# One core, chunk-selecting attention with a softplus layer: another order of all operations in the order table

## Chip, cores and metric

One core of one Trainium2 chip runs the whole program. The metric is the device time of one execution in microseconds (us). The kernel before was timed in 3 runs: median 256.69 us, lowest 255.29, highest 258.97. The shares, durations and waits below come from one further execution that the hardware profiler recorded.

## What is computed

Attention over 4 batches, 8 heads, 768 positions and 64 elements per head, in which each query sees only 6 chunks of 32 keys, and then a two-layer network with softplus over the 3072 tokens:

```python
k_min, k_max = k_chunks.min(axis=3), k_chunks.max(axis=3)
ub = sum(maximum(q * k_min, q * k_max), axis=-1)      # bound of each query and chunk
ub = where(causal, ub, -1e9)
top_chunks = argsort(ub, axis=-1)[..., -6:]
scores = where(selected & causal, q @ k.T / 8, -1e9)
attn = softmax(scores)
x = (attn @ v) as 3072 tokens x 512
h = x @ w_in                                          # 512 x 2048
out = softplus(h) @ w_out                             # 2048 x 512
```

Inputs and output are float32 in HBM; the matmuls run on bfloat16.

## The kernel before

The 12 blocks (4 batches, three thirds of 256 positions) go through the same stages, and the stages of neighbouring blocks are mixed on every engine.

- Loads. Block 0's k and q come as float32 halves on SP's queue (L377, tile wx) and are cast on ScalarE or VectorE (L294, L295). All other q, k and v halves (L364), w_in in four pieces (L392) and w_out in four pieces (L399) are issued by GpSimd on the software queue, which converts them to bfloat16 on the way. These issues stand in GpSimd's own instruction stream, between its causal selects (L715) and copies.
- Preparation of a block n. k and q are transposed: on TensorE for blocks 0 to 2 (L481), by DMA transposes on SP from block 3 on (L485). VectorE takes the maximum and minimum of each chunk (L508 from PSUM, L500 from the DMA's tile), writes them into BD (L295) and splits q into its positive and negative part (qpos, qneg: L557 on ScalarE, L559 and L561 on VectorE). TensorE forms the bounds ub (L580, L584). VectorE adds the causal term (L592), finds the sixth largest (L603, L607) and writes the mask (L622, L625). The mask is transposed (L637, L643 on TensorE; L646 by DMA from block 3 on) and copied beside q (L295 or L294, "mc" in the table).
- Attention. Scores on TensorE (L697, L698, "s"), exponential on ScalarE (L705, "ex"), the causal select of the diagonal chunk on GpSimd (L715, "af"), the product with v on TensorE (L727, "av"), normalisation on VectorE (L737, L738, "nm"), then the transposed x by TensorE (L753) or by DMA (L742).
- Network. x times w_in (L891, "h"), softplus as exponential and logarithm on ScalarE (L896, L901), times w_out: plainly for blocks 0 to 3 and 11 (L921, "y"), with seven products of quarter blocks (L836) for blocks 4 to 10. For the seven products sums of parts of w_out are made first (L795, "wd", "wh", "wv", on VectorE or GpSimd). Results leave through SP's queue (L872, L933).

No scheduler decides the order. The string ORDER (L201) lists 1576 words. The first letter of a word is the engine (P TensorE, A ScalarE, V VectorE, G GpSimd, S SyncE), the rest the operation with its block; `#i` picks one of several of the same name. A word `z30` is filler on TensorE: 30 // 4 matmuls of 512 columns and 30 % 4 of 128 columns on a zero tile (L1007, L1009). Each engine runs its own words in the order of the table, and buffers are handed out in that order too (Plan.in_order):

```python
o.eng = {"P": "PE", "A": "ACT", "V": "DVE", "G": "POOL", "S": "SP"}[word[0]]
assert o.eng in o.engines and not o.wait, word
for b in o.alloc:
    _, b.pool, b.slot = min((s.since, p, i) for p in b.pools for i, s in enumerate(p.slots) if not s.taken)
```

A DMA that must wait for another operation waits at its issuing engine, and everything behind it on that engine waits too.

Of the kernel before, what the change touches and what calls it, by code (L numbers as in the profile page):

```python
# [206 lines left out]
Gw_in0 z45 Ps0 Ps0#6 Aex0#6 Aex0 Amc0 z3 Pub1 Ps0#4 Gw_in1 Aex0#4 Vqac1 Vkc1#1 Vmx1 Vraw1 z1 Ps0 Aex0 z16 Ps0 PqT2
PkT2 Ps0 Vqc2 Gaf0#2 Gaf0 Gaf0#4 Gaf0 Vkc1 z4 PmT1 Pav0#2 z12 Pav0#3 Vnm0#1 Gld_v1.0 Gld_v1.1 z14 Pav0 Pav0 Gw_in2
Aex0 Aex0 Amc1 PkT2 Ps1#4 Ps1 PoT0#1 Gld_q3.0 Gaf0 Gaf0 Amc1 Vqpn2 Vqpn2 Vnm0 Aex1#4 z8 Ps1#3 PoT0 Aex1 Aex1#3 Gaf1#1
Gaf0 Gld_q3.1 z2 Ps1#5 Aex1#5 Vkx2 Vkn2 Axc0 Pav0 Pav0 Ps1#7 Aex1#7 Vnm0 Axc0 Vbd2 z4 Ps1#6 Aex1#6 Vkc2 z6 Ps1 Aex1  # L210
Gaf1 Gw_in3 z6 PoT0 Pav0 Pav0 Vnm0 Ps1#8 Ps1#12 Aex1#8 Aex1#12 Pub2 PoT0 Ps1 Vkc2 Axc0#3 Axc0 Vmx2 Vraw2 Ps1 Aex1#9
Aex1 z2 Ph0 Ps1#13 Aex1#13 Pav1 Ps1#14 Aex1#14 Pav1 Gaf1 Ps1#11 PmT2 Ps1#15 Gw_out0 Aex1#11 Ae0 Aex1#15 Gaf1 Vqac2
Vmc2 Gaf1#6 Ph0 Ae0 Ps1 Ps2 Vnm1 Ph0 Aex1 Aex2 Ps2#2 Aex2#2 Vmc2 Gld_v2.0 Gld_v2.1 Pav1 Pav1 PoT1 Gaf1#7 Gld_k3.0
Ps2#6 Vnm1 Ae0 Ps2#5 Aex2#6 Aex2#5 Ph0#4 Ae0#4 Gaf1 Ps2#4 Pav1#6 Ps2#18 Pav1#7 Aex2#18 Aex2#4 Gvone Gld_k3.1 Gaf1
Gw_out1 Gw_out2 Gaf2#1 Ph0#5 Ae0#5 Gw_out3 Gaf2 Vxc1 Vnm1#3 PoT1 SkD3 Pav1 Ps2 PoT1#3 Ps2#23 Ph0 Aex2#23 Aex2 Vxc1 Ae0
Aln0 Ph0 Ps2 Ps2#12 Pav1 Vxc1#3 Vnm1 Aex2 Ph0 Ps2#13 Aex2#12 Ae0 Aex2#13 PoT1 Vxc1 Py0 SqD3 Ae0 Ps2#8 Aln0 Pav2 Ps2#11
# [827 lines left out]
```

## Time and profile before

| | |
|---|---|
| median of 3 runs (lowest to highest) | 256.69 us (255.29 to 258.97) |
| the profiled execution's own time | 256.73 us |
| its span, first to last instruction | 255.0 us |
| TensorE matmul busy | 247.9 us (97%), 2786 matmuls |
| ScalarE, VectorE, GpSimd busy | 215.6, 177.7, 115.6 us (85, 70, 45%) |
| share of 16 DMA engines: software queue, hardware queue | 73.5%, 32.1% |
| granted TensorE clock | 1.00 in every stretch |

A matmul's busy time runs from its issue to its modelled end, so matmuls that follow each other overlap, and the mean duration of one is longer than the distance to the next. Idle time of TensorE is what counts here; idle time of another engine counts only where TensorE waits for it.

### The profile page before, as it was taken

How to read it: one execution, taken by the hardware profiler on the slowest of the kernel's cores; microseconds unless marked ns; L12 is line 12 of the kernel's file. 1: busy time of each engine (PE TensorE's matmuls, PEld its weight loads, DVE VectorE, ACT ScalarE, POOL GpSimd, SP SyncE). 2: the span in 40 equal slices, each digit the busy share in tenths (PEclk: the TensorE clock that was granted, in tenths of full speed). 3: DMA queues.
4: the chain of work that ended last, by engine and by line, in shares of the span. 5: the costliest groups of instructions: out<-in, count | busy, mean ns of one | idle time of the engine just before them, and what ended most of it. 6: DMA issues, size and time to landing. Idle time of an engine off the chain costs nothing.

```text
span 255.0 us, 7155 instructions
## 1 busy us (share of the span) xinstructions
PE 247.9 (97%) x2786; PEld 202.4 (79%) x2786; DVE 177.7 (70%) x562; ACT 215.6 (85%) x396; POOL 115.6 (45%) x196
## 2 busy tenths in 40 slices
PE   6999999999999999999999999999999999999995
PEld 2666798775686777877789999899999988999873
DVE  5899952059899677987898995977765554535501
ACT  3889999987799998997998989999899997767661
POOL 6689791870885774861643732633012213200020
PEclk9999999999999999999999999999999999999999
DMA  7999999999999899999999989568422440200213
GB/s 177 131 111 170 181 195 189 153 116 182 158 134 148 139 172 127 157 146 159 90 162 102 115 152 190 63 50 60 101 66 64 43 146 3 82 3 4 82 44 123
DMA packets 114722, 29.90 MB, mean 117 GB/s; under 512 B 104544, under 2 KB 111712, under 8 KB 114688
## 3 DMA queue, kind: packets, MB, share of 16 engines
q0 software_dynamic: 74944, 13.11, 73.5%
q1 hardware_dynamic: 39744, 16.33, 32.1%
q8 instruction: 22, 0.36, 0.6%
q14 instruction: 12, 0.10, 0.1%
HBM read 27.26 MB, written 6.29 MB: 132 GB/s over the span
## 4 chain that ended last, share of the span: by engine, by line
PE 80%; DVE 9%; DMA 6%; ACT 3%; issue 1%; SPq 0%
PE ph L891 28%; PE py L921 9%; PE pt L836 9%; PE py L836 8%; PE ps L697 5%; DMA qt<-io 5%; PE po L727 5%; PE ps L698 4%; PE pt L727 2%; PE ph L921 2%; PE pt L697 2%; DVE kx L508 2%; PE pt L580 2%; PE pt L698 1%; DMA wx<-in_k_dram 1%; DVE qa L295 1%
## 5 line engine op out<-in xcount | busy, mean ns | idle before, releaser
L891 PE MATMUL ph<-x,w_in_sb 128*128 128x256 bf16 x768 | 97.6, 272 | 0.0
L705 ACT ACTIVATE pt<-ps 128x512 bf16<-128x512 f32 (+1 forms) x151 | 78.1, 551 | 10.0 <-PE ps L698 9.2
L715 POOL TENSOR_SCALAR_AFFINE_SELECT pt<-pt 128x256 bf16<-128x256 bf16 x96 | 39.1, 427 | 98.9 <-ACT pt L705 94.7
L891 PEld LDWEIGHTS <-w_in_sb 128*128 128x128 bf16 x768 | 72.9, 98 | 9.6 <-issue 0.2
L896 ACT ACTIVATE e<-ph 128x512 f32<-128x512 f32 x96 | 56.6, 607 | 8.3 <-PE ph L891 7.9
L901 ACT ACTIVATE g<-e 128x1024 bf16<-128x1024 f32 x48 | 50.5, 1062 | 0.3
L921 PE MATMUL py<-w_out_sb,g 128*128 128x512 bf16 (+1 forms) x144 | 34.0, 367 | 0.0
L727 PEld LDWEIGHTS <-pt 128*128 128x128 bf16 x672 | 27.7, 97 | 2.7
L921 PEld LDWEIGHTS <-g 128*128 128x128 bf16 x176 | 16.2, 97 | 11.1
L705 ACT ACTIVATE pt<-pt 128x512 bf16<-128x512 f32 (+1 forms) x41 | 22.3, 556 | 3.0 <-PE pt L698 2.5
L836 PEld LDWEIGHTS <-g 128*128 128x128 bf16 x224 | 21.0, 98 | 2.3
L727 PE MATMUL po<-v,pt 128*128 128x65 bf16 x468 | 22.5, 193 | 0.0
L500 DVE TENSOR_REDUCE kx<-kT 128x32 bf16<-128x1024 bf16 x18 | 21.3, 1210 | 1.2 <-DMA kT<-io 1.1
L364 POOL DMA_DIRECT2D v<-in_v_dram x24 | 21.4, 895 | 0.2
L364 POOL DMA_DIRECT2D io<-in_k_dram x22 | 20.0, 910 | 0.3
L364 POOL DMA_DIRECT2D io<-in_q_dram x22 | 19.9, 905 | 0.3 <-issue 0.3
L697 PE MATMUL ps<-qt,kb 128*128 128x256 bf16 x76 | 20.0, 272 | 0.0
L697 PE MATMUL ps<-qa,ka 96*128 96x256 bf16 x75 | 19.7, 273 | 0.3 <-DVE qa L295 0.3
L698 PE MATMUL ps<-qt,kb 128*128 128x128 bf16 (+1 forms) x76 | 18.1, 245 | 0.0
L698 PE MATMUL ps<-qa,ka 96*128 96x256 bf16 (+1 forms) x75 | 17.7, 244 | 0.0
L836 PEld LDWEIGHTS <-df 128*128 128x128 bf16 x168 | 15.9, 98 | 2.0
L1007 PE MATMUL py<-zero 128*128 128x512 bf16 x52 | 15.3, 411 | 1.1 <-DVE zero L304 1.1
(127 smaller groups left out, 409.0 us busy)
## 6 DMA issues: line engine op xcount, KB each, us to landing
out_dram<-ysb SPq DMA_DIRECT2D x23, 256.0 KB, 2.3
v<-in_v_dram POOLq DMA_DIRECT2D x24, 128.0 KB, 5.5
io<-in_k_dram POOLq DMA_DIRECT2D x22, 128.0 KB, 5.6
io<-in_q_dram POOLq DMA_DIRECT2D x22, 128.0 KB, 5.4
w_in_sb<-in_moe_w_in_dram POOLq DMA_DIRECT2D x4, 512.0 KB, 8.8
w_out_sb<-in_moe_w_out_dram POOLq DMA_DIRECT2D x4, 512.0 KB, 11.6
wx<-in_k_dram SPq DMA_DIRECT2D x2, 256.0 KB, 3.2
wx<-in_q_dram SPq DMA_DIRECT2D x2, 256.0 KB, 4.3
```

The costliest lines, as they stand in the source:

```text
L364: lambda e, t=t: nc.gpsimd.dma_start(out=into(nm, n, t), in_=rows(nm, n, t)),
L500: nc.vector.tensor_reduce(kx.ap[:, :, j].rearrange("d p (t c) -> d t p c", t=NT), kT.ap.rearrange("d p x -> d (p x)").rearrange("d (t p c ...
L697: nc.tensor.matmul(sp.ap[:, 0:QB], kk[0:nr, p, j * 128:(j + 1) * 128], qq, start=True, stop=True)
L698: nc.tensor.matmul(sp.ap[:, QB:w], kk[0:nr, p, (j + 1) * 128:(j + 2) * 128], qq[:, 1] if last else qq, start=True, stop=True)
L705: lambda e, sp=sp, pt=pt, h=h, j=j, w=w: nc.scalar.activation(pt.ap[:, h, j:j + 2].rearrange("k j c -> k (j c)")[:, 0:w], sp.ap[:, 0:w], A ...
L715: nc.gpsimd.affine_select(out=d, in_=d, compare_op=ALU.is_ge, fill=0.0, base=0, channel_multiplier=-1, pattern=[[0, 2], [1, 128]])
L727: nc.tensor.matmul(o[:, u, h], pt.ap[:, h, j, c0:c0 + 128], T.V[i][:, j, 2 * p + h, :], start=(j == 0), stop=(j == t0 + u))
L836: nc.tensor.matmul(bank.ap[:, c * HD:(c + 1) * HD], a(f), w(f), start=start and f == 0, stop=f == HF - 1, skip_group_check=True)
L891: nc.tensor.matmul(o[:, j], T.w_in[:, dt, ft * 128:(ft + 1) * 128], x.ap[:, dt], start=(dt == 0), stop=(dt == KDM - 1))
L896: lambda e, hb=hb, eb=eb, f2=f2: nc.scalar.activation(eb.ap[:, f2 * 512:(f2 + 1) * 512], hb.ap, ACT.Exp),
L901: lambda e, eb=eb, g=g, f4=f4: nc.scalar.activation(g.ap[:, f4 * 4:(f4 + 1) * 4].rearrange("f j c -> f (j c)"), eb.ap, ACT.Ln, bias=1.0),
L921: nc.tensor.matmul(yb.ap[:, 0:c1 - c0], g.ap[:, f, u * 128:(u + 1) * 128], T.w_out[:, f, c0:c1], start=(f == 0), stop=(f == KFF - 1))
```

## The change

The text of ORDER is replaced; nothing else is. All operations of the old table are in the new one, with the same buffer pools and dependencies; what differs is their order on each engine, which engine does some of them, and the filler. The table now has 1579 words:

```diff
 ORDER = """
-Vzero Vbd0#1 Vcm0 Vkb0 Gident Vr4 Gc4 Sld_k0.1 Vbd0 Vmr0 Gld_k1.0 Gld_q1.0 Sld_k0.0 Acast_k0.0 z30 PkT0 Vmr0 PkT0
-Gld_q1.1 Gld_k1.1 Gcm Gld_q2.0 Gvone Sld_q0.0 Vkx0 Vcast_k0.1 z24 PkT0 PkT0 Vkx0 Vkn0#1 Acast_q0.0 PqT0 PqT0 Aqc0
...
+Vzero Gvone Gident Sld_k0.1 Vkb0 Vmr0#1 Vbd0 Vmr0 Sld_k0.0 Sld_q0.1 Vr4 Gc4 Gld_q1.0 Gvone Vcast_k0.0 z30 PkT0 PkT0
+Vkx0 Vcast_k0.1 z24 PkT0 PkT0 Sld_q0.0 Vkn0 Vkx0 Vkn0 Vcm0 Voh Acast_q0.0 Gld_q1.1 Gld_k1.0 Gld_k1.1 Acast_q0.1 PqT0
...
```

Counted over the table: filler words 22 with a sum of 238 before, 25 with a sum of 231 now, that is 52 matmuls of 512 columns and 30 of 128 before, 48 and 39 now. VectorE has 302 operations before and 310 now, ScalarE 393 and 385, GpSimd 189 and SyncE 95 in both. The first cast of k, three copies of x of block 2 and one or two small copies of the output in blocks 2, 4, 6 and 7 go from ScalarE to VectorE; halves of qpos/qneg and of the mask copies go both ways; the sums of w_out and the last additions of the output trade places between VectorE and GpSimd.

VectorE (DVE), the start of the program, from the constants to the first mask. kx is the tile of chunk maxima and minima of k, io the cast input, ph and pt PSUM tiles, qpos and qneg the parts of q. Before:

```order
L316 COPY rows_67<-ident 128x128
L325 MEMSET bd_76 128x192
L324 MEMSET mraw_78 128x256
L324 MEMSET mraw_79 128x256
L508 TENSOR_REDUCE kx_103<-ph_87 128x2x8
L295 CAST io_97<-wx 128x4x2x64
L508 TENSOR_REDUCE kx_103<-ph_88 128x2x8 x2
L306 SCALAR_TENSOR_TENSOR ohb<-ident 32x768
L508 TENSOR_REDUCE kx_103<-ph_87 128x2x8
L561 TENSOR_SCALAR qpos_109<-qt_106 128x512
L295 COPY kb_74<-ph_88 64x2x256
```

Now:

```order
L316 COPY rows_67<-ident 128x128
L295 CAST io_96<-wx 128x4x2x64
L508 TENSOR_REDUCE kx_103<-ph_87 128x2x8
L295 CAST io_96<-wx 128x4x2x64
L508 TENSOR_REDUCE kx_103<-ph_87 128x2x8
L508 TENSOR_REDUCE kx_103<-ph_88 128x2x8 x2
L310 MEMSET cmask 128x4
L306 SCALAR_TENSOR_TENSOR ohb<-ident 32x768
L561 TENSOR_SCALAR qpos_109<-qt_106 128x512
L295 COPY qa_105<-qt_106 64x512
L295 COPY qt_106<-pt_92 128x512
```

All three memsets of bd and mraw stand ahead of rows now; both casts of k are VectorE's, and the four maxima and minima stand ahead of the one long operation that builds ohb.

GpSimd (POOL), from v of block 1 to the weights. v_70, io_101 and io_102 are the targets of v, q and k halves, pt the probabilities that the causal select works on. Before:

```order
L364 DMA v_70<-in_v_dram 128x8x64 x2
L392 DMA w_in_sb<-in_moe_w_in_dram 128x4x512
L364 DMA io_101<-in_q_dram 128x8x64
L715 AFFINE_SELECT pt_116<-pt_116 128x2x128
L715 AFFINE_SELECT pt_115<-pt_115 128x2x128
L715 AFFINE_SELECT pt_113<-pt_113 128x2x128
L715 AFFINE_SELECT pt_115<-pt_115 128x2x128
L364 DMA io_101<-in_q_dram 128x8x64
L715 AFFINE_SELECT pt_113<-pt_113 128x2x128
L392 DMA w_in_sb<-in_moe_w_in_dram 128x4x512
L715 AFFINE_SELECT pt_114<-pt_114 128x2x128
L399 DMA w_out_sb<-in_moe_w_out_dram 128x4x512
```

Now, from the third k half on:

```order
L364 DMA io_101<-in_k_dram 128x8x64
L364 DMA v_70<-in_v_dram 128x8x64
L715 AFFINE_SELECT pt_115<-pt_115 128x2x128 x2
L399 DMA w_out_sb<-in_moe_w_out_dram 128x4x512
L311 AFFINE_SELECT cmask<-cmask 128x4
L364 DMA io_102<-in_q_dram 128x8x64
L715 AFFINE_SELECT pt_113<-pt_113 128x2x128
L364 DMA io_102<-in_q_dram 128x8x64
L715 AFFINE_SELECT pt_113<-pt_113 128x2x128
L715 AFFINE_SELECT pt_114<-pt_114 128x2x128
L399 DMA w_out_sb<-in_moe_w_out_dram 128x4x512 x2
```

Both q halves of block 3 stood between pieces of w_in; they now stand behind the second piece of w_out. The second and third piece of w_in, further ahead, now stand together behind v of block 1, where the third stands in the rows of before.

VectorE between the mask of block 3 and its copy beside q. wv, wd and wx are the sums of w_out, kx the chunk maxima of block 4, rec and osb the normalisation of block 2, mT the transposed mask. Before:

```order
L625 CAST mraw_79<-ub_112 128x16
L795 TENSOR_TENSOR wd<-w_out_sb 128x512
L795 TENSOR_TENSOR wv<-w_out_sb 128x1024
L795 TENSOR_TENSOR wx<-w_out_sb 128x512
L795 TENSOR_TENSOR wd<-w_out_sb 128x512
L500 TENSOR_REDUCE kx_103<-kT_94 128x2x4x4 x2
L737 RECIPROCAL rec_124<-po_90 128x4
L738 TENSOR_TENSOR osb_123<-po_90,rec_124 128x256
L295 COPY qa_107<-mT_138 32x2x2x128 x2
```

Now:

```order
L625 CAST mraw_79<-ub_112 128x16
L795 TENSOR_TENSOR wv<-w_out_sb 128x1024
L737 RECIPROCAL rec_120<-po_90 128x4
L738 TENSOR_TENSOR osb_119<-po_90,rec_120 128x256
L795 TENSOR_TENSOR wd<-w_out_sb 128x512
L295 COPY qa_107<-qt_108 64x1024
L500 TENSOR_REDUCE kx_103<-kT_94 128x2x4x4 x2
L737 RECIPROCAL rec_124<-po_90 128x4
L738 TENSOR_TENSOR osb_123<-po_90,rec_124 128x256
L295 COPY bd_77<-kx_103 64x8x8 x2
L561 TENSOR_SCALAR qpos_109<-qt_106 128x1024
L295 COPY qa_107<-mT_138 32x2x2x128 x2
```

Two sums have left this stretch; a normalisation, the copy of q, the copies into bd and qpos of block 4 have come in.

## Rows read from the trace of the kernel before

**Rows 1.** TensorE's waits: line waited for: us in total, times, longest.
```profile
PE ph L481 <- ACT io L294: 1.1, 1, 1.1
PE py L1007 <- DVE zero L304: 1.1, 1, 1.1
PE pt L580 <- DVE qneg L559: 0.8, 2, 0.5
PE ps L697 <- DVE qa L295: 0.3, 1, 0.3
PE pt L697 <- DVE qa L295: 0.2, 1, 0.2
PE pt L643 <- DVE mraw L625: 0.2, 1, 0.2
```
**Rows 2.** Busy time by stretch; the first number is the stretch's length.
```profile
core 0: us, PE busy (x) PEld busy (x) DVE busy (x) ACT busy (x) POOL busy (x), PEclk, DMA share, GB/s
10.00:20.00 10.00, 9.67 (x127) 6.62 (x125) 9.55 (x42) 8.93 (x17) 8.83 (x16) 1.00 1.30 113
...
50.00:60.00 10.00, 9.40 (x98) 6.36 (x96) 6.37 (x14) 9.31 (x17) 5.90 (x9) 1.00 2.17 122
...
100.00:120.00 20.00, 20.00 (x260) 16.71 (x257) 17.50 (x55) 17.68 (x33) 11.91 (x20) 1.00 1.56 151
...
240.00:255.00 15.00, 11.96 (x94) 8.94 (x92) 2.48 (x5) 7.00 (x11) 1.45 (x2) 1.00 0.28 106
```
**Rows 3.** The filler: the narrow ones by line, then three stretches of the timeline.
```profile
L1009 PE MATMUL py<-zero 128*128 128x128 bf16 x30 | 4.0, 219 | 0.0
...
5.54 1.46 PE L1007 MATMUL py<-zero 128*128 128x512 bf16 x6
...
14.26 2.55 PE L1007 MATMUL py<-zero 128*128 128x512 bf16 x11
...
17.03 0.33 PE L1009 MATMUL py<-zero 128*128 128x128 bf16 x3
```
**Rows 4.** TensorE's timeline: third h group, bound of block 3, first scores of block 3.
```profile
33.28 1.04 PE L891 MATMUL ph<-x,w_in_sb 128*128 128x256 bf16 x8
...
58.46 0.18 PE L580 MATMUL pt<-bd,qneg 128*128 128x16 bf16 x1 [0.48 <-DVE qneg L559]
...
68.46 0.27 PE L697 MATMUL ps<-qa,ka 96*128 96x256 bf16 x1
```
**Rows 5.** GpSimd's timeline: third w_in piece, second q half of block 3, w_out.
```profile
22.15 0.77 POOL L392 DMA_DIRECT2D w_in_sb<-in_moe_w_in_dram  x1
...
25.77 0.89 POOL L364 DMA_DIRECT2D io<-in_q_dram  x1
...
36.12 1.51 POOL L399 DMA_DIRECT2D w_out_sb<-in_moe_w_out_dram  x2
```
**Rows 6.** DMA issues, us to landing: all w_in; those issued 25.77, 36.12, 44.90.
```profile
w_in_sb<-in_moe_w_in_dram POOLq DMA_DIRECT2D x4, 512.0 KB, 8.8
...
io<-in_q_dram POOLq DMA_DIRECT2D x1, 128.0 KB, 7.8
...
w_out_sb<-in_moe_w_out_dram POOLq DMA_DIRECT2D x1, 512.0 KB, 9.7
...
qt<-io SPq DMA_TRANSPOSE x1, 12.4
```
**Rows 7.** SyncE's timeline: the transpose of q of block 3.
```profile
44.90 4.51 SPq L485 DMA_TRANSPOSE qt<-io  x1
```
**Rows 8.** VectorE's timeline between the mask of block 3 and its copy.
```profile
62.06 0.20 DVE L625 CAST mraw<-ub 128x16 bf16<-128x16 f32 x1
...
63.74 2.35 DVE L500 TENSOR_REDUCE kx<-kT 128x32 bf16<-128x1024 bf16 x2
...
67.44 0.94 DVE L295 COPY qa<-mT 32x512 bf16<-32x512 bf16 x2
```
**Rows 9.** GpSimd's load issues by line, 0 to 64 us: ns min/median/max of one.
```profile
L364 POOL DMA_DIRECT2D io<-in_k_dram x10: 873/893/1054, 3.0 to 52.8; - x10
```

More of the change, by code (lines that the diff above doesn't have):

```diff
@@ L207 @@
[L207 to L216, printed above, removed]
@@ new lines @@
+Gld_v1.0 PqT2 z1 Ps0 Aex0 z7 PmT1 Amc1 Sohk Gld_v1.1 Gaf0 Vqc2 Pav0 z9 Pav0 Vnm0 Amc1 z14 PoT0 Pav0#4 Pav0#5 Vkc1
+Vnm0#2 Ps1#4 Aex1#4 Vqpn2 Ps1#12 PkT2 Aex1#12 Vqpn2 z3 Pav0 Pav0 Vnm0 PkT2 Ps1#6 Gw_in1 Aex1#6 Gw_in2 z4 Ps1#15
+Aex1#15 Gaf0#7 Gaf0 Gaf1#7 Vkx2 Vkn2 z6 Ps1#13 Aex1#13 z3 Ps1#5 z5 Ps1 Aex1#5 z2 Ps1 Gld_k3.0 Pav0 PoT0#2 Pav0 Axc0
+Aex1 Aex1 z4 Ps1 Aex1 Vbd0 Gaf1 PoT0 Vbd2 Ps1#7 Axc0#2 Aex1#7 Vkc2 Gw_out0 Vnm0 z8 Ps1 Pub2 Aex1 PoT0 Ps1 Ps1#11 Vkc2
+Axc0 Axc0 Ph0 Aex1 Vmx2 Gw_in3 Gaf1 Gaf1 Gld_v2.0 Gaf1 Gaf1#6 Aex1#11 Ps1#10 Pav1 Ps1#14 Pav1 Ae0 Vraw2 Vnm1 Aex1#14
@@ new lines @@
+Aex2#23 Ps2 Ph1 Gld_q4.0 Aex2 Ps2#13 Ph1#5 Gld_q4.1 Aln0 Gwh0 Gld_k5.0 Gld_k5.1 Vwh2#1 Ps2 Py0 Aex2#13 Aex2 SkD4
+Ps2#16 Ae1 Aex2#16 Aln0 Ps2 Pav2 Pav2 Vnm2 Ps2#21 Aex2 Ph1#4 Vkx3 Vkn3 Py0 Ps2#22 Vwd0 Aex2#21 Ae1#4 Aex2#22 Ae1#5
+PoT2 Vxc2 Vbd3 Ps2 Pav2 Pav2 Ps2 Vkc3 Vwh6#1 Py0 Ph1 Aye0 Vqpn3 Vkc3 Sohk Py0 Ph1 Py0 Vxc2 Ae1 Aln1 Py0 Aqpn3 Pub3
+Vwv2 Aln1 Py0 Vuba3 Vmx3 Aln1 Aye0 Ph1 Aex2 Vraw3 Gwd2 Gaf2#7 Py1 Py1 Py1 SqD4 Vwv4 Ae1 Ae1 Aln1 Py1 Vnm2 Aex2 SmD3
+Gaf2 Gld_v3.0 Aye1 Vwd4 Vqac3 Vkx4 Pav2 Pav2 Vkn4 Gld_v3.1 PoT2 Axc2 Vnm2 Vbd4 Vqpn4 Sohk Skb0 Py1 Py1 Vmc3 Aqpn4 Pub4
@@ new lines @@
+Py3 Pav5 Vnm5 Vkc7 Ae4 Aex5 Ae4 Ps6 Gaf5 Vqpn7 Vqpn7 Ps6 Ps6#4 Ph4#3 Aex6 Aex6 Aex6 Gaf6 Ps6#6 Aex6#6 Ph4 Ps6 Aex6
+Gaf6#3 Aln3 Pav5 Pav5 Ps6#7 Aex6#7 Pub7 SkD9 Gld_q9.1 Gaf6#6 Vnm5 Vuba7 Vmx7 Vraw7 Py3 Gaf6#7 Gaf6 Gld_q8.0 Ae4 Ae4
+Aln4 Py3 Aye3 Ph4 SxD5 SxD5#3 Gaf6 Ae4 Vqac7 Sst1 SxD5 SxD5 Ps6 Aex6 Aex6 Vkx9 Vkn9 Ph4#6 Pav6#2 Pav6#3 Vnm6#1 Vkc9
+Ae4#6 Ph4#7 Py3 Pav6#6 Pav6 Pav6#7 Vnm6#3 SmD7 Ph4 Aln4 SqD9 Ae4#7 Gaf6#5 Gaf6 Gld_q11.0 Gld_k8.1 Pav6 Gld_k10.0
+Gld_q8.1 Py3 Ph5#4 Vnm6 Vmc7 Vmc7 Vdl4 Ps7#13 Ps7#12 Aln4#3 Ae4 Aln4 Gld_v9.0 Py3 Ps7#8 Ps7#10 Ph5#5 Pav6 Pav6 Aex7#8
@@ new lines @@
+Py5#12 Py5#13 Py5 Py5 Vmc8 Vmc8 Ps8#18 Pav9#5 Aex8#18 Aye5 Vyv5 Vnm9#2 Vyc5 Ph7#6 Ps8#19 Pav9 Pav9 Ps8 Ps8#6 Py5
+Ps8#23 Py5 Aln6 Aex8#6 Aex8 Ps8#2 Vnm9 Ae7#6 Ayd5 SkD10 Vkx10 Vdl6 Vyw5 Vyx5 Aex8#23 Pav9 Aex8#19 Vyf5 Ph7#4 Pav9
+Ps8#12 Ph7 Aex8#2 SqD10 Vde6 Vqpn10 Vqpn10 Vdh6 Vkn10 Vkx11 Ps8#17 Ps8#11 Vnm9 Py6 Ae7 Ps8#5 SxD9 SxD9#3 SxD9 SxD9
+Sst5#1 Aex8#12 Aex8#5 Aex8#11 Ae7#4 Aex8#17 Gaf8#1 Gaf8 Gld_v8.0 Ph7#7 Gld_v8.1 Gld_v11.0 Gaf8#5 Gld_q11.1 Gld_v11.1
+Gaf8#3 Ps8#4 Ps8 Ps8#9 Py6 Py6 Aex8#9 Ps8#14 Aex8 Ps8#22 Ph7#5 Ae7#7 Aex8#4 Aex8#22 Ae7#5 Aex8#14 Py6#4 Py6#5 Ps8#13
```

127 lines of the change are left out of this document (58 added, 69 removed).

## The prediction

> **What bounds the kernel now.** I read the time first: the profiled execution took 256.73 us, of which 255.0 are its span, and the median of the three runs is 256.69, so the sum can be made against 256.73 and taken for the median as it stands. Then the waits of TensorE. They come to 3.7 us in seven waits [rows 1]; 2.2 of these are the start, the zero tile and the first cast of k. Inside the program 1.5 us are left: three waits in the preparation of a block (qneg twice, 0.8; mraw once, 0.2) and two at the first scores of a block, which wait for the mask's copy (0.3 and 0.2). The busy time by stretch says the same from the other side: TensorE is idle 0.33 us of 10 to 20, 0.60 of 50 to 60, nothing of 100 to 120 [rows 2], and 3.04 of the last 15, which is the last copy and store after the last matmul. So TensorE's stream bounds the kernel from end to end, and no other engine counts except where it makes this stream wait. The work in the stream is the same in both tables. What can change is the filler, which is work on TensorE only because the table says so, the waits, and the start and the end.
>
> **The change part by part.**
>
> Filler. Wide fillers come to the same distance in every stretch: eleven take 2.55 us and six take 1.46, so five more take 1.09, 0.218 each. Narrow ones: three take 0.33 and one alone 0.219, so 0.055 each [rows 3]. Before there are 52 and 30, now 48 and 39: 4 x 0.218 less and 9 x 0.055 more, a gain of 0.87 - 0.50 = 0.37 us. A filler runs whether anything is late or not, so this is certain unless its place turns into a wait.
>
> Start. TensorE's first steps are in both tables the same 30, two transposes, 24, and so is the first transfer that they wait for. On VectorE bd and mraw are cleared before rows and not after, so GpSimd's first select and with it its first load come about 0.6 us later; the loads behind it are needed only by block 1. The cast of k that gates the first transposes goes from ScalarE to VectorE at the same length within 0.01 us, and VectorE has nothing else to do then. All maxima are then done before the long ohb operation; in exchange qc of the second half stands on VectorE, and the last q half to be issued is cast first on ScalarE. I take a new wait of 0.25 us at the first bound, between 0 and the 1.1 us that the cast of k costs today [rows 1], because the queue of VectorE is shorter by the maxima and longer by a copy.
>
> Block 1 and 2. The wait of block 1's bound for qneg is 0.3 (0.8 less the longest, 0.5), that of block 2's mask transpose for mraw 0.2 [rows 1]. In the new table one of qpos and qneg of block 1 is ScalarE's and the other is ahead of the maxima on VectorE, and block 2's mask transpose stands behind more scores. Both waits go: 0.5 less. What is late next is the copy of the mask, and the bound is that a wait of the same size comes back, so between 0.5 and 0.
>
> Weights. The second piece of w_in now goes out where the third did, at 22.15 [rows 5]. With the median 8.8 us to landing [rows 6] it is there at 30.95; its first user today, the third h group, starts at 33.28 [rows 4], and stands at the same place in the new stream within 0.6 us (the same filler, 0.37 less, and fewer waits). There is cover of 2 us, and I cost it at nothing; were GpSimd that much later, each us beyond it would be a us of TensorE.
>
> q of block 3. Its second half is issued at 25.77 and lands after 7.8 us, at 33.6, long before SyncE wants it: the transpose of q is issued at 44.90, behind that of k, and lands 12.4 later, at 57.3 [rows 5 to 7]. Then VectorE splits q and TensorE waits until 58.46, 0.48 us [rows 4]. Now the q halves are behind the second piece of w_out and the k halves are ahead of it. If q is on time, the wait stays; TensorE comes 1.0 us later, for one more y group (4 x 0.218 = 0.87) and a score pair stand ahead of the bound, and the split is divided between ScalarE and VectorE. If it is not, that is the first rival. I take no change: nearest to the row of today.
>
> Masks of blocks 3 to 5. VectorE ends the mask at 62.26 and the copy beside q at 68.38; the first scores start at 68.46, so this queue just misses being a wait [rows 4, 8]. The four sums behind the mask take 1.48 us (62.26 to 63.74). In the new order two of them are gone and a normalisation, a copy of q, two small copies and a qpos have come in, each 0.4 to 0.6 by rows of the same kind: some 1.2 us more work, against 0.7 us in which VectorE is idle today and about 1.3 us that the mask starts earlier, since one normalisation and the sums ahead of it have moved. TensorE meanwhile gets there about 1.3 us sooner (one y group, one score pair and two products with v less, one bound more). The two sides come to a wait between 0 and 0.8 us; I take 0.2. At blocks 4 and 5 the 0.5 us of today stays: work between bound and scores grows by 0.3 and shrinks by 0.4.
>
> More on VectorE, less on ScalarE. Eight operations move, some 4 us; in 100 to 120 VectorE is busy 17.50 of 20 and TensorE never waits [rows 2], so nothing is added.
>
> GpSimd's issues beside VectorE. Over the first 64 us ten issues of k halves took 873 to 1054 ns, with 893 in the middle [rows 9], while VectorE was busy 9.55 of 10 us [rows 2]: at worst 0.16 us more for one. The Trainium skill, "SBUF — State Buffer", section "SBUF: two separate sides", says that GpSimd cannot write its descriptors while a VectorE operation holds the port pair that they share; by that each cast or copy moved to VectorE could hold up a load for its whole length. The rows show no such length here, and by the rule the sum would change only if a load were late already.
>
> End. The last two y groups, the last copy and the last store are of the same kinds in the same order. Stores of blocks 8 and 9 now queue behind those of block 10 on SyncE; TensorE's stream ends 3.04 us before the span does in either case. Zero, up to 0.5 if these stores meet the last one.
>
> Sum: 256.73 - 0.37 - 0.5 + 0.25 + 0.2 = 256.3 us.
>
> **The rivals.**
>
> The q halves late (slower). If the software queue delivers in the order of issue, the second q half lands behind the second piece of w_out: 36.12 + 9.7 + 2 x 0.89 = 47.6 [rows 5, 6]. SyncE then issues q's transpose 2.7 us later than at 44.90, and so does all behind it; at 12.4 to landing the bound of block 3 starts at about 61.2 and not 58.46. Of these 2.7 us 1.0 is work that now stands ahead, so the stream is 1.7 behind today's where the forecast has it 0.6 ahead (0.37 + 0.5 - 0.25): price 2.3. With the wait of the block's mask at its upper end, 0.6 more, 256.3 + 2.9 = 259.2. It decides from the point where q lands after 44.90. For it: the order of GpSimd's issues. Against it: all weights start earlier in the new queue, and the 12.4 us may be the price of sharing the engines with weights, which are then nearer their end.
>
> All waits gone (faster). The new places could cover all of the 1.5 us, with no new wait: 256.73 - 0.37 - 1.5 = 254.9. For it: each wait is under 0.5 us, and a single group of matmuls put ahead of it is 0.87. Against it: at blocks 4 and 5 the distance from bound to scores hardly grows.
>
> The change does not do what it says (no difference). The start waits for the first k half and the last q half as before, and waits move rather than go: 256.4 to 257.0. For it: the first transposes, their cast and their transfer are the same on every queue.
>
> **How the numbers follow.** The forecast of 256.3 with its own small terms (255.6 to 256.9) has 0.4, the case of no difference 0.2, all waits gone 0.2, the late q halves 0.15; 0.05 is left for a wait that I have not seen. Two per cent is 5.1 us, about what a measurement of this kernel can tell from no change. A gain of that size would need more than the 0.37 of filler, the 1.5 of waits and the 1.1 of the first cast together: 0.02. A loss of that size needs the late q halves and as much again: 0.06. Within 2%: 0.92. The range goes from 253.8, a little over 1 us below all waits gone for the scatter of the runs (they lie 1.4 below and 2.3 above their median), to 259.7, the late q halves and 0.5 of scatter.
>
> **What would show it right or wrong.** Right: TensorE's waits name no qneg of block 1 and no mraw; wide fillers are 48 at 0.218; TensorE is idle under 0.2 us of 10 to 20; the bound of block 3 starts within 1.5 us of 58.46; the scores of block 3 wait less than 0.8. Wrong: a wait of TensorE over 1 us anywhere after the first cast, above all at L580 with a DMA of io behind it, or h groups waiting for w_in; or a last store that ends more than 3.5 us after the last matmul.

## The result, and the profile after

The changed kernel took 260.38 us (median of six runs, 258.53 to 260.80) beside 256.95 us for the kernel before (six runs, 255.29 to 260.45): a ratio of 1.0112, 95% interval 1.0069 to 1.0155. It is 1.1% slower; by 2% the two count as the same. Ratios and intervals, here and below, leave out the runs more than 1.5% above the fastest of their kernel; medians and ranges take all. The prediction had 256.3 and a range up to 259.7, so time and range were missed. The profiled execution took 260.51 us with a span of 258.8, 3.78 us over the profiled execution before.

TensorE's waits in the changed kernel (answers to [rows 1]; line waited for: us in total, times, longest):
```profile
PE po L727 <- DVE osb L738: 1.2, 2, 0.7
PE pt L697 <- DVE qt L295: 1.1, 1, 1.1
PE py L1007 <- DVE zero L304: 1.1, 1, 1.1
PE ph L481 <- DVE io L295: 0.9, 1, 0.9
PE ps L697 <- DVE qa L295: 0.6, 1, 0.6
PE pt L697 <- DVE qa L295: 0.3, 1, 0.3
PE ph L643 <- DVE mraw L625: 0.2, 1, 0.2
PE pt L753 <- DVE osb L738: 0.2, 1, 0.2
```
The waits at the start come to 2.0 us, 0.2 less than before. The seven others come to 3.6 us where the kernel before had five with 1.5. The qneg waits are gone; new are a wait of 1.1 us for a copy of a mask (qt, L295) and two, 1.2 us together, for a normalisation of VectorE (osb, L738).

The busy time by stretch says where they stand (answers to [rows 2]):
```profile
core 0: us, PE busy (x) PEld busy (x) DVE busy (x) ACT busy (x) POOL busy (x), PEclk, DMA share, GB/s
10.00:20.00 10.00, 10.00 (x126) 6.70 (x125) 8.68 (x37) 8.47 (x15) 7.97 (x12) 1.00 1.37 118
...
50.00:60.00 10.00, 10.00 (x107) 7.13 (x105) 6.79 (x15) 8.69 (x16) 6.03 (x7) 1.00 1.89 168
...
80.00:100.00 20.00, 18.42 (x209) 13.95 (x207) 17.46 (x48) 16.62 (x34) 14.28 (x21) 1.00 1.53 146
100.00:120.00 20.00, 18.64 (x243) 14.86 (x241) 13.22 (x55) 16.62 (x33) 8.71 (x16) 1.00 1.17 119
```
10 to 20 and 50 to 60, where the prediction had counted idle time, are now full. TensorE is idle in 80 to 100 (1.58 us, block 5's scores) where the prediction had let blocks 4 and 5 keep 0.5 us between them, and in 100 to 120 (1.36 us, block 6's), where it had added nothing.

Block 5 in the timeline of the changed kernel (start us, us, engine, line; VectorE, then GpSimd, then TensorE):
```profile
90.35 1.88 DVE L295 COPY qa<-mT 32x512 bf16<-32x512 bf16 x2
92.24 2.47 DVE L295 COPY qt<-mT 32x512 bf16<-32x512 bf16 x2
...
94.97 0.42 DVE L738 TENSOR_TENSOR osb<-po,rec 128x256 bf16<-128x256 f32 x1
...
90.34 1.77 POOL L364 DMA_DIRECT2D v<-in_v_dram  x2
92.11 0.43 POOL L715 TENSOR_SCALAR_AFFINE_SELECT pt<-pt 128x256 bf16<-128x256 bf16 x1
92.47 0.90 POOL L364 DMA_DIRECT2D v<-in_v_dram  x1
93.38 2.34 POOL L795 TENSOR_TENSOR wx<-w_out_sb 128x512 bf16<-128x512 bf16 x2
...
93.53 0.28 PE L697 MATMUL pt<-qt,kb 128*128 128x256 bf16 x1 [1.10 <-DVE qt L295]
...
95.44 0.58 PE L727 MATMUL po<-v,pt 128*128 128x65 bf16 x14 [0.47 <-DVE osb L738]
```
Read it engine against engine. Four copies of the mask, 32 x 512 each, take 4.35 us. Of all 32 such copies of this execution the median is 0.29 us. GpSimd issues three loads and forms two weight sums (wx, L795) over the same 5 us; the change has moved these two sums from VectorE to GpSimd and put them here. The normalisation at 94.97 is not slow (0.42, as everywhere): it is queued behind the copies. By piece, the copies are:
```profile
L295 DVE COPY qa<-mT x2: 284/924/1565, 90.3 to 90.7; 32x512 bf16<-32x512 bf16 x2
L295 DVE COPY qt<-mT x2: 1206/1220/1235, 92.2 to 93.5; 32x512 bf16<-32x512 bf16 x2
```
and the same four copies in the kernel before:
```profile
L295 DVE COPY qa<-mT x2: 679/702/725, 91.4 to 92.1; 32x512 bf16<-32x512 bf16 x2
L295 DVE COPY qt<-mT x2: 288/404/521, 93.5 to 94.0; 32x512 bf16<-32x512 bf16 x2
```
Minimum, median and maximum in ns. The second copy ends at 90.67 + 1.57 = 92.24, 0.13 after the second load's issue (90.34 + 1.77 = 92.11). The third ends at 93.47, 0.10 after the next load's issue (93.37). The fourth ends at 94.72, 0.16 after the first of the two sums (94.56).

Block 6 (VectorE, SyncE, TensorE):
```profile
111.54 0.58 DVE L295 COPY qa<-mT 32x512 bf16<-32x512 bf16 x2 [3.15 <-DMA mT<-mraw]
...
112.77 0.42 DVE L738 TENSOR_TENSOR osb<-po,rec 128x256 bf16<-128x256 f32 x1
...
105.27 1.19 SPq L646 DMA_TRANSPOSE mT<-mraw  x1
...
112.18 0.27 PE L697 MATMUL ps<-qa,ka 96*128 96x256 bf16 x1 [0.61 <-DVE qa L295]
...
113.25 0.46 PE L727 MATMUL po<-v,pt 128*128 128x65 bf16 x10 [0.74 <-DVE osb L738]
```
Here the copies are short. The mask's transpose, issued at 105.27, was landed only at 111.5. VectorE stood idle for 3.15 us, and a normalisation that needed no mask waited behind the copies in its queue. TensorE waited for both in turn.

The distance was no shorter than before. In the kernel before the same transpose and the first scores behind it (SyncE, TensorE) read
```profile
102.54 1.19 SPq L646 DMA_TRANSPOSE mT<-mraw  x1
...
108.86 0.27 PE L697 MATMUL ps<-qa,ka 96*128 96x256 bf16 x1
```
TensorE comes to the scores 6.3 us after the transpose's issue in both kernels (now it does so at 111.57, where its wait begins). What grew is the time from issue to landing, before and now:
```profile
mT<-mraw SPq DMA_TRANSPOSE x1, 4.1
...
mT<-mraw SPq DMA_TRANSPOSE x1, 6.2
```

The start (TensorE; the changed kernel):
```profile
5.31 0.61 PE L481 MATMUL ph<-ident,io 128*128 128x128 bf16 x4 [0.86 <-DVE io L295]
5.71 2.76 PE L1007 MATMUL py<-zero 128*128 128x512 bf16 x6
...
31.47 0.71 PE L891 MATMUL ph<-x,w_in_sb 128*128 128x256 bf16 x5
```
Six wide fillers took 2.76 us, where the same six before took 1.46 [rows 3]: TensorE still ran at the lower of its two clock levels (1.2 GHz) and came to 2.4 GHz only near 10 us. The granted clock reads 1.00 over these stretches in both kernels; it is the length of equal matmuls that shows the level. Up to 5.3 us the instructions of TensorE are the same in both kernels, and up to 4.0 us both run at the lower level (0.43 us from one wide filler to the next).

### The profile page after: what moved, and what is told of

Read it like the earlier page. It is cut to its first block, busy times and chain, and to the rows that moved or that the text cites. A ratio compares the mean times of both kernels' runs of the same rounds, so it can differ in the third digit from the quotient of the medians.

```text
span 258.8 us, 7151 instructions
## 1 busy us (share of the span) xinstructions
PE 249.9 (97%) x2791; PEld 204.0 (79%) x2791; DVE 179.8 (69%) x568; ACT 214.0 (83%) x390; POOL 118.4 (46%) x196
## 4 chain that ended last, share of the span: by engine, by line
PE 82%; DVE 11%; DMA 4%; issue 1%; SPq 0%; ACT 0%; DVEq 0%; ACTq 0%
PE ph L891 28%; PE py L921 10%; PE pt L836 9%; PE py L836 7%; PE po L727 5%; PE ps L697 5%; PE ps L698 4%; PE py L1007 3%; DMA mT<-mraw 2%; PE pt L697 2%; PE pt L727 2%; DVE qa L295 2%; PE pt L580 1%; PE ph L921 1%; PE pt L698 1%; DMA wx<-in_k_dram 1%
## 5 line engine op out<-in xcount | busy, mean ns | idle before, releaser
L715 POOL TENSOR_SCALAR_AFFINE_SELECT pt<-pt 128x256 bf16<-128x256 bf16 x96 | 41.1, 447 | 98.5 <-ACT pt L705 90.1
L705 ACT ACTIVATE pt<-ps 128x384 bf16<-128x384 f32 (+1 forms) x143 | 75.4, 554 | 11.0 <-PE ps L698 9.9
L921 PE MATMUL py<-w_out_sb,g 128*128 128x512 bf16 x144 | 35.8, 379 | 0.0
L705 ACT ACTIVATE pt<-pt 128x384 bf16<-128x384 f32 (+1 forms) x49 | 27.0, 561 | 3.2 <-PE pt L698 3.0
L727 PE MATMUL po<-v,pt 128*128 128x65 bf16 x510 | 23.7, 193 | 1.3 <-DVE osb L738 1.2
L737 DVE RECIPROCAL rec<-po 128x4 f32<-128x4 f32 x37 | 6.6, 178 | 22.2 <-PE po L727 22.0
L697 PE MATMUL ps<-qt,kb 128*128 128x256 bf16 x74 | 19.8, 272 | 0.0
L697 PE MATMUL ps<-qa,ka 96*128 96x256 bf16 x69 | 18.2, 273 | 0.7 <-DVE qa L295 0.6
L698 PE MATMUL ps<-qt,kb 128*128 128x256 bf16 (+1 forms) x74 | 17.9, 246 | 0.0
L1007 PE MATMUL py<-zero 128*128 128x512 bf16 x48 | 16.1, 455 | 1.1 <-DVE zero L304 1.1
```

What stands on the lines that cost most here:

```text
L697: nc.tensor.matmul(sp.ap[:, 0:QB], kk[0:nr, p, j * 128:(j + 1) * 128], qq, start=True, stop=True)
L698: nc.tensor.matmul(sp.ap[:, QB:w], kk[0:nr, p, (j + 1) * 128:(j + 2) * 128], qq[:, 1] if last else qq, start=True, stop=True)
L705: lambda e, sp=sp, pt=pt, h=h, j=j, w=w: nc.scalar.activation(pt.ap[:, h, j:j + 2].rearrange("k j c -> k (j c)")[:, 0:w], sp.ap[:, 0:w], A ...
L715: nc.gpsimd.affine_select(out=d, in_=d, compare_op=ALU.is_ge, fill=0.0, base=0, channel_multiplier=-1, pattern=[[0, 2], [1, 128]])
L727: nc.tensor.matmul(o[:, u, h], pt.ap[:, h, j, c0:c0 + 128], T.V[i][:, j, 2 * p + h, :], start=(j == 0), stop=(j == t0 + u))
L921: nc.tensor.matmul(yb.ap[:, 0:c1 - c0], g.ap[:, f, u * 128:(u + 1) * 128], T.w_out[:, f, c0:c1], start=(f == 0), stop=(f == KFF - 1))
```

## The experiments

Theories. A: the late rise of the clock is chance and no part of the change; A2: TensorE's idle time before the first cast lets it happen. B: a mask copy that meets GpSimd's instructions waits for their end, and the change has put loads and sums beside block 5's copies. C: block 6's second wait is only the order of VectorE's queue. The rivals stand in each expectation. The edits are to the order table alone; where words of one engine are shown, the other engines' words between them are left out.

**Both kernels again.** Nothing edited.

> The changed kernel once more, nothing edited, for a second look at its start and as the base of the runs beside it. Theory A (the later rise of TensorE's clock in the first profile, about 10 us against 5.5 us in the kernel before, is chance and not the change): in this profile the rise may lie anywhere between 5 and 11 us, and the span moves with it by up to 2 us. Rival (the changed start causes it): the rise lies at 9 to 11 us again. By both, the waits of blocks 5 and 6 come back: near 1.1 and 0.5 us in block 5 (93 to 96 us), near 0.6 and 0.7 us in block 6 (112 to 114 us). Time 259 to 261 us, ratio to the kernel before 1.007 to 1.016.

> The kernel before once more, for a second look at its start. Theory A (the rise is chance): the clock rises at another time than 5.5 us in at least some executions of this kernel, and then the time lies 1 to 2.5 us above 256.7. Rival (the order of the start sets it): the rise lies at 5.5 us again and the time is 255.3 to 257.5.

The changed kernel took 259.23 us (ten runs), beside 258.14 for the kernel before on the same chip (25 runs, 255.73 to 261.11): ratio 1.0041, interval 0.999 to 1.0092. Its second profile took 258.25 us, with
```profile
5.58 1.46 PE L1007 MATMUL py<-zero 128*128 128x512 bf16 x6
...
29.74 1.03 PE L891 MATMUL ph<-x,w_in_sb 128*128 128x256 bf16 x8
```
The same order has the full clock from 5.6 us here, and its first h group starts 1.73 us sooner. So the late rise is no fixed effect of the change. Block 5's two waits were there again; block 6's were not, its mask having landed in 3.8 us and not 6.2. (That one is the exception: in the twelve other profiles of this order and its edits the mask took 4.9 to 6.2 us, in the three of the kernel before 3.9 to 4.1. What on the queues makes the difference is not shown.) TensorE waited 0.8 us for w_out instead. The kernel before had the early clock again, against what A expected of it (of the 25 runs beside it four were under 256.8 and seven over 259.5: it scatters as much), and in its second profile a wait of 1.0 us for an attention output's transpose, which the first did not have.

**Block 5: GpSimd's loads and sums later.**
```diff
-Gld_v5.0 Gld_v7.0 Gaf4 Gld_v6.0 Gwh4 Gwh6 Gld_q7.1 Gld_v5.1 Gaf5#5
+Gaf4 Gaf5#5 Gld_v5.0 Gld_v7.0 Gld_v6.0 Gwh4 Gwh6 Gld_q7.1 Gld_v5.1
```


> GpSimd's five value and query loads and its two weight sums that ran at 90.3 to 97.5 us stand behind a select that runs at 97.5 us, so that GpSimd does little while VectorE copies block 5's mask. Theory B (a mask copy that starts while GpSimd issues a load or forms a sum ends only 0.1 us after GpSimd's instruction): the four copies of block 5 take 0.3 us each instead of up to 1.57, the two waits of block 5 (1.10 and 0.47 us in the first profile) go, and the time falls by 1 to 1.6 us, to 258.8 to 259.4. Rival (the mask lands too late because the order leaves less work between bound and scores): the copies still end at 92 to 94.7 us, both waits stay, no change of time. The risk in both: the loads that are moved arrive 6 us later, which could show as a new wait in blocks 6 or 7.

258.31 us (ten runs), 0.9 under the changed kernel beside it; ratio 1.0033, 1.0000 to 1.0066, not clear of the 1.0041 there. The copies:
```profile
L295 DVE COPY qa<-mT x2: 285/418/550, 90.5 to 91.1; 32x512 bf16<-32x512 bf16 x2
L295 DVE COPY qt<-mT x2: 283/284/286, 91.4 to 91.7; 32x512 bf16<-32x512 bf16 x2
```
1.4 us in place of 4.35, the first one 0.55 beside a select. Both waits of block 5 are gone, though the mask was transposed no sooner (issued at 86.96, in the changed kernel at 86.82). That is B against its rival. The profile had the late clock and block 6's waits, so its own time of 258.65 says little.

**Block 6: the normalisation first.** Words of VectorE:
```diff
-Vmc6 Vbd7 Vnm5
+Vnm5 Vmc6 Vbd7
```


> One normalisation of block 5 on VectorE (a reciprocal and a product) stands ahead of block 6's first mask copies instead of behind them. Theory C (the wait of 0.74 us at 113.2 us is there only because this normalisation is queued behind copies that wait for a mask transpose): that wait goes, the wait for the mask at 112.2 us (0.6 us) stays or grows by up to 0.7 as TensorE comes to the scores as early as before, and the time falls by 0.5 to 0.8 us. Rival (TensorE's next work waits for the mask anyway, so the wait only changes its name): the wait for the mask grows by what the other loses, no change of time.

257.60 us (ten runs); ratio 1.0002, 0.9965 to 1.0039. From VectorE's timeline:
```profile
107.04 0.43 DVE L738 TENSOR_TENSOR osb<-po,rec 128x256 bf16<-128x256 f32 x1
109.39 0.58 DVE L295 COPY qa<-mT 32x512 bf16<-32x512 bf16 x2 [1.93 <-DMA mT<-mraw]
```
The normalisation is done 1.9 us ahead of the copies, and the wait for it in block 6 is gone; the mask was late again (5.6 us to landing), but not so late that TensorE waited. Over all profiles of the changed order: with the normalisation behind, seven of eight have that wait (0.4 to 0.7 us); with it ahead, none of five. The medians differ by 1.6 us from the changed kernel's, more than a wait of 0.7 gives; the rest I take for scatter.

**Block 5 in halves.** Sums later (twice, the second time with a single run):
```diff
-Gld_v5.0 Gld_v7.0 Gaf4 Gld_v6.0 Gwh4 Gwh6 Gld_q7.1 Gld_v5.1 Gaf5#5
+Gld_v5.0 Gld_v7.0 Gaf4 Gld_v6.0 Gaf5#5 Gwh4 Gwh6 Gld_q7.1 Gld_v5.1
```


> GpSimd's two weight sums of block 5 (and the two loads queued behind them) stand behind a select of 97.5 us; its value loads stay beside VectorE's mask copies. Theory B (a mask copy ends 0.1 us after the GpSimd instructions that it meets): the first copy still takes 1.5 us beside two loads and the third about 1.2 beside a select and a load, so TensorE's wait of 1.1 us for the third stays; the fourth falls from 1.2 to 0.3 us, and the wait of 0.5 us for the normalisation behind it goes. Time 0.5 to 0.7 us under the changed kernel. Rival (only the sums, which use VectorE's kind of arithmetic, hold the copies, and load issues do not): first and third copy shorten too, both waits go, 1.6 us.

> The third experiment once more, for its profile alone. There the second mask copy of block 5 took 0.67 us and the wait of 1.1 us was gone too, though the two loads beside it stood at the same times against it as in the changed kernel, where it took 1.56 in four profiles of four. If which of GpSimd's loads the copy waits for is chance, it may take 1.56 us here; if it goes by the order (by what is queued behind the loads), it takes 0.67 again.

Loads later, sums in place:
```diff
-Gld_v5.0 Gld_v7.0 Gaf4 Gld_v6.0 Gwh4 Gwh6 Gld_q7.1 Gld_v5.1 Gaf5#5
+Gaf4 Gwh4 Gwh6 Gaf5#5 Gld_v5.0 Gld_v7.0 Gld_v6.0 Gld_q7.1 Gld_v5.1
```


> The other half of the first block 5 experiment: GpSimd's loads that ran at 90.3 to 97.5 us stand behind the select of 97.5 us, and the two weight sums stay where they are, so that they now meet the mask copies with no load ahead of them. Theory B (a copy that meets a sum waits for its end): the second copy ends 0.1 us after the first sum, at about 1.1 us long, the third 0.1 us after the second sum, at about 1.1 us, and the fourth takes 0.3; TensorE's wait for the third copy falls from 1.1 to about 0.8 us, the wait behind the fourth goes, and the time is 0.6 to 1.0 us under the changed kernel. Rival (loads alone hold the copies): all copies at 0.3 to 0.6 us and both waits gone, 1.6 us.

Sums alone later, with loads still queued in their place:
```diff
-Gld_v5.0 Gld_v7.0 Gaf4 Gld_v6.0 Gwh4 Gwh6 Gld_q7.1 Gld_v5.1 Gaf5#5
+Gld_v5.0 Gld_v7.0 Gaf4 Gld_v6.0 Gld_q7.1 Gld_v5.1 Gaf5#5 Gwh4 Gwh6
```


> The third experiment with only the two weight sums moved behind the select of 97.5 us: the query load and the value load that stood behind them stay, so that after the first loads of block 5 GpSimd goes straight on with two more. If the long second mask copy (1.56 us) comes from whatever GpSimd has ready behind its loads, it takes 1.56 us again, and TensorE's wait of 1.1 us comes back. If it comes from the sums alone, it takes 0.67 and the wait is gone, as in the third and eighth experiments.

Sums later: 257.62 us (ten runs, 1.0026, 0.998 to 1.0072) and 255.79 (one). Loads later: 259.19 (ten runs, 1.0049, 1.0015 to 1.0083). Sums alone: 258.12 (one). None of these times is clear of the unedited order's 1.0041 (0.999 to 1.0092); what follows rests on the profiles. The profile with the sums later, VectorE and GpSimd:
```profile
89.23 0.99 DVE L295 COPY qa<-mT 32x512 bf16<-32x512 bf16 x2
90.23 0.87 DVE L295 COPY qt<-mT 32x512 bf16<-32x512 bf16 x2
...
89.22 1.78 POOL L364 DMA_DIRECT2D v<-in_v_dram  x2
```
and with the loads later, the two engines and TensorE:
```profile
90.15 3.09 DVE L295 COPY qa<-mT 32x512 bf16<-32x512 bf16 x2
...
90.51 2.26 POOL L795 TENSOR_TENSOR wx<-w_out_sb 128x512 bf16<-128x512 bf16 x2
...
92.98 0.27 PE L697 MATMUL pt<-qa,ka 96*128 96x256 bf16 x1 [1.40 <-DVE qa L295]
```
With the sums beside it, one copy took 2.78 us of those 3.09, from 90.15 to 92.93, across a select and both sums (the sums end at 92.77). I had expected it to get its turn between two sums, and two copies of 1.1; it got none, and this half alone costs a wait of 1.4 us. With the loads beside it, the second copy took 0.67 us and the fourth 0.56, each to 0.1 us behind the end of a load's issue, and both waits were gone, the 1.1 too, against my expectation. The second profile repeated that, and so did the run with loads queued in the sums' place (0.67 and 0.56). So: 1.56 us in four profiles of four with the sums in the queue behind the loads, 0.67 in three of three without them, though the two loads start within 0.02 us of the same times against the copy in all seven. In this order the sums are what costs. In the kernel before a sum stood behind the two loads as well, and its copies got their turn between them (0.68 and 0.73 us), so a sum in the queue is not enough by itself. How a sum that starts 2.7 us after the copy makes it miss the turn between two loads is open.

**The start: filler up to the cast.**
```diff
-Acast_k0.0 z30 PkT0
+Acast_k0.0 z38 PkT0
```
That is the kernel before's line; in the changed kernel the word is the same z30.

> The changed kernel with 38 instead of 30 units of filler ahead of the first transposes (two wide matmuls more), so that TensorE is hardly idle before the first cast. In the profiles so far the full clock came between 3.7 and 5.3 us in four executions, and at about 10 us in the two in which it had not come when TensorE fell idle at 4.2 us. Theory A2 (TensorE's idle time of 0.9 to 1.1 us ahead of the first cast is what puts off the rise in some executions, in both kernels): the rise comes by 5.5 us, the span of the profile is that of the early kind, and over the timed runs the median falls by 0.4 to 1.2 us with fewer runs above 260. Rival (the rise is chance whatever TensorE does there): the spread of the times stays as it was, and the median within 0.4 us of the changed kernel's; if the extra filler delays the first transposes, up to 0.4 us slower.

> The kernel before with the same longer filler ahead of its first transposes. Theory A2: the start's cost is common to both kernels and no part of the change, so this one gains as much as the changed kernel does: median 0.4 to 1.2 us under the kernel before. Rival (the changed start alone has the late rise): no gain here, within 0.3 us.

On the changed kernel: 258.66 us (12 runs, 257.55 to 259.82), ratio 1.0044, 1.0015 to 1.0074. On the kernel before: 257.48 (12 runs, 255.80 to 258.51), ratio 0.9993, 0.9956 to 1.0031, beside 35 unedited runs of 255.21 to 260.69. In both the slow end of the scatter is cut: of the 35 unedited runs 14 lie above 259 us, of the 12 with the longer filler none. (The changed order was not run unedited beside these.) The profiles show it better, by the start of the first h group: over the eight profiles of the changed order with 30 units it lies between 29.74 and 31.62 us, over the five with 38 between 29.91 and 30.07, the first of which reads
```profile
30.07 1.03 PE L891 MATMUL ph<-x,w_in_sb 128*128 128x256 bf16 x8
```
So the late rise is no fixed effect of this order, and A2 fits: by the length of the wide fillers the clock was full by about 7 us in all five (TensorE idle for 0 to 0.6 us before the cast), and later, up to 10 us, in four of the eight with 30 units, in which it stood idle for 0.6 to 1.1 us. Thirteen profiles make this likely and no more. That the kernel before has the late rise too is inferred from its slow runs: neither of its two profiles with 30 units shows it. The medians settle less: 0.8 us under the kernel before, with no change at all inside the interval. With this scatter out of both, the changed order was 1.2 us slower, both measured together (258.66 against 257.48): that is nearer to what the change itself costs than the 3.4 us of the first comparison.

**All three moves together**, measured twice.

> The changed kernel with the moves of the first two experiments together (GpSimd's loads and sums behind block 5's mask copies, the normalisation ahead of block 6's) and the longer filler. If theories A2, B and C hold, their gains add up: 1.6 us of block 5, 0 to 0.8 of block 6 and 0.4 to 1.2 of the start, 255.5 to 257 us, 0.3 to 0.8% under the kernel before. Rival (the waits come back elsewhere, since what follows is fixed by landings): not under 257.5 us.

> The kernel of the fifth experiment once more (0.9952 of the kernel before there, 0.9914 to 0.999). If theories A2, B and C hold it lies at 0.991 to 0.998 of the kernel before again; if that was the chip or chance, at 0.998 to 1.003.

256.28 us (12 runs) against 258.31, ratio 0.9952, interval 0.9914 to 0.999; then 256.50 (12 runs) against 258.73, ratio 0.9957, 0.9922 to 0.9991. That is some 0.45% under the kernel before. The longer filler is not what does it: beside the first of the two, the kernel before with the same filler took 257.48, 1.2 us more, and the changed kernel with it 258.66, so that the moves of blocks 5 and 6 are worth 2.4 us. The first of the two profiles:
```profile
80.00:100.00 20.00, 20.00 (x221) 15.34 (x218) 16.64 (x51) 18.37 (x39) 13.26 (x20) 1.00 1.37 134
100.00:120.00 20.00, 19.71 (x254) 15.59 (x253) 15.98 (x63) 17.72 (x33) 12.41 (x23) 1.00 1.57 146
```
The two stretches that lost 2.94 us in the changed kernel lose 0.29. The second profile had a wait of another kind,
```profile
PE py L921 <- DMA w_out_sb<-in_moe_w_out_dram: 2.0, 2, 1.5
```
which three of the 13 profiles of this order and its edits have (0.3 to 2.0 us) and none of the kernel before. The prediction held w_out for safe; it is not always.

**Blocks 3 and 4 cleared too.** The kernel with all three moves, and in the first run also two sums of VectorE moved; words of GpSimd, then of VectorE:
```diff
-Gld_q6.0 Gld_q5.0 Gaf3#2
+Gaf3#2 Gld_q6.0 Gld_q5.0
...
-Gld_k6.0 Gld_k6.1 Gaf4#6
+Gaf4#6 Gld_k6.0 Gld_k6.1
...
-Vwv4 Vnm2 Vwd4
+Vnm2
...
-Vraw4
+Vraw4 Vwv4 Vwd4
```


> The kernel of the fifth experiment, and the same treatment of blocks 3 and 4: two query loads of 66.8 us and two key loads of 77.4 us each stand one select later, and two weight sums of VectorE (0.7 and 0.4 us) that stood ahead of block 4's bound stand behind it. By theory B the operations of VectorE at 67.0 (0.9 us), 67.97 (0.72) and 78.6 us (0.56) fall to 0.42, 0.29 and 0.29, and TensorE's waits of 0.26, 0.22, 0.16 and 0.40 us at 67.5 to 77.5 us shrink: 0.4 to 1.0 us under the fifth experiment, 255.3 to 255.9 us. Rival (these waits are set by the mask transposes' landings, not by VectorE): within 0.2 us of the fifth experiment. Risk: key and query loads that arrive 2 to 3 us later.

> The ninth experiment with the two weight sums of VectorE left where the changed kernel has them: only the loads beside the mask copies of blocks 3 and 4 stand later. Theory B: the operation of VectorE at 67.0 us falls from 0.90 to 0.42, the mask copies at 68 and 78.6 us from 0.72 and 0.56 to 0.3; TensorE's waits at 67.5 and 77.5 us (0.26, 0.22, 0.16, 0.40) shrink by 0.3 to 0.8 in all, 0.2 to 0.8 us under the eleventh experiment. Rival: they are set by the work ahead of them on VectorE or by the masks' landings, no difference to the eleventh.

The first took 258.70 us (12 runs, 1.0020, 0.9985 to 1.0056), the second, without the last two edits, 258.02 (12 runs, 1.0044, 1.0 to 1.0089), 1.5 us over the kernel with three moves beside it. Both miss what was expected. VectorE's operations fell as B says (the one at 67.0 us from 0.90 to 0.43, the mask copies of block 3 to 0.3), and TensorE's delays of 0.26, 0.22 and 0.16 us went (counted from start to start; as idle time they were under 0.1 us each). But each run had a new wait, here of the first and of the second:
```profile
78.07 0.34 PE L727 MATMUL po<-v,pt 128*128 128x65 bf16 x6 [1.47 <-DVE osb L738]
```
```profile
PE pt L580 <- DVE qpos L561: 1.5, 1, 1.5
...
PE pt L580 <- DVE qneg L559: 0.7, 1, 0.7
...
84.00:90.00 6.00, 6.00 (x46) 3.37 (x42) 3.65 (x23) 2.10 (x5) 2.47 (x6) 0.72 1.11 93
```
In the first the two sums, 1.1 us, now stand ahead of a normalisation, and behind them two copies of k (kb and ka, 0.42 us each in the kernel with three moves) took 1.38 and 0.82 us beside GpSimd's selects and a load: the copies have met other instructions. In the second VectorE stood idle for 1.71 us until block 5's query, loaded later, was transposed, and after waits of 1.5 and 0.7 us TensorE's granted clock was 0.72 over the next 6 us (1.00 in the first run's same stretch): the wait cost twice. Five of the 12 runs have a granted clock of 0.993 over the whole execution, and they are the five slowest.

## Why the prediction was wrong

The 3.78 us between the two profiled executions: 1.73 of clock at the start (31.47 against 29.74 in the other profile of the same order), 3.6 - 1.5 = 2.1 of waits inside, -0.2 of waits at the start, -0.37 of filler. That is 3.3. Some 0.3 of the rest is that a wait costs more than its idle time, which is counted from the modelled end of the matmul before: at 112.18 the next matmul starts 0.78 us later than it would at the usual distance, its idle time is 0.61, and inside the program there are two waits more than before. The last 0.2 I have not followed.

That the median fell outside the range is in part scatter: 1.73 of the 3.78 us come and go with the clock at the start, and in the second comparison the same kernel took 259.23, inside the range. That would have been luck, since the sum has neither the clock nor the waits of blocks 5 and 6 in it.

- Filler, -0.37: right in kind. The trace has 48 wide and 39 narrow ones; their busy time can't be compared, since many ran at the lower clock.
- Start, +0.25: failed both ways. No wait came at the first bound (10 to 20 is full). What the sum had no term for is the clock. The rows of one execution [rows 3] showed the early kind, and I took it for the kernel's own. The median of three runs in 255.29 to 258.97 was the warning that one execution does not carry a difference of 1 us.
- Blocks 1 and 2, -0.5: -0.3 came (no qneg). The 0.2 for mraw stayed, now at block 1's mask (21.8 us, ph in place of pt).
- Weights, 0: right for w_in. w_out was late in three of 13 profiles.
- Query of block 3, no change: better than that. Its transpose was issued at 47.83, 2.9 us later than in [rows 7], as the rival of the late halves said, but it landed in 8.6 us and not in 12.4 [rows 6], so the bound did not wait at all. (It began at 60.69, though, and not within 1.5 us of 58.46.) The rival's order of queues was right and its price wrong: the transpose takes 12.2 to 12.4 us to land in three profiles of the kernel before and 8.5 to 11.0 in thirteen of the changed order, so 12.4 was the price in the old order and no fixed one. Why it is shorter now is not shown.
- Scores of block 3, +0.2: no wait is named there. "At blocks 4 and 5 the 0.5 us of today stays" is the first step that failed: block 4 kept 0.3, block 5 came to 1.1 + 0.5. It counted TensorE's work between bound and scores and let the copies between them keep their length; those of block 5 went from some 2.2 us to 4.3.
- "More on VectorE, less on ScalarE: nothing is added" is the second. 100 to 120, which "never waits", lost 1.36 us in the first profile. The mistake is to read a stretch of one order as a property of the stretch. Block 6's mask has the same 6.3 us from the issue of its transpose to its scores as before, but it lands in 4.9 to 6.2 us and not in 4.1, and a normalisation stands behind its copies. The sum gave block 6 no term.
- "GpSimd's issues beside VectorE" is the third, and the cause of block 5's waits. I asked only whether VectorE holds up a load [rows 9]. The row that answered the other question was in the trace before: the first two copies of block 5 took 0.68 and 0.73 us there, beside two loads, against a median of 0.29. The page of the Trainium skill that I weighed, "SBUF — State Buffer", section "SBUF: two separate sides", states it in both directions: whichever of the two engines starts first keeps the port pair for its whole instruction and "the other fully blocks". The trace agrees on the direction that I left out: copies of 0.29 us took 1.2 to 2.8 to the end of GpSimd's sums. It differs in one point: most mask copies that started up to 0.23 us after the start of a load's issue still ran in 0.28, while those that started 0.26 to 0.64 us after it mostly ended 0.1 us behind its end or behind the next load's, so a load need not hold the pair from its first moment. (At one place, 138 to 145 us, a copy that started 0.12 us into a load, 0.21 in the kernel before, was held as well, in every profile; why is open.) The same section's condition, that of VectorE's operations only those in a two-port mode or with two inputs from SBUF contend, fits too: the products that read float32 from PSUM kept their 0.42 us beside every GpSimd instruction.
- End, 0: right. TensorE ends 3.1 us before the span, before 3.04.

"A wait of TensorE over 1 us anywhere after the first cast" was named as what would show the prediction wrong, and it did, though at L697 and not at L580. That the change stays within 2% held; the sign of the forecast did not.

## What to carry to other kernels

When work is moved to an idle GpSimd, look at what VectorE copies at that moment: here bf16 copies from SBUF to SBUF stood still until GpSimd's load issue, select or sum had ended, sometimes until two or three in a row had, and everything behind them in VectorE's queue stood still too. Put what needs no transfer ahead of what waits for one. And before a difference of 1% is read from two profiles, look in several executions for how much of it is the clock at the start.

## What was not expected of the hardware

- A VectorE copy of 0.29 us waited through three GpSimd instructions in a row (2.78 us) without a turn between them.
- The same mask transpose at the same place of the same order landed after 6.2 us in one execution and 3.8 in another; the kernel before has it in 3.9 to 4.1.
- With TensorE idle for about 1 us at 4.2 us, its full clock came anywhere from there to 10 us over eight profiles of the changed order; with two wide fillers more (idle for 0 to 0.6 us) it came by about 7 us, and the first h group started within 0.16 us in all five profiles.
